# Attention scores from 128-row products instead of pairs of 64-row ones, on one Trainium2 core

## The chip, the cores and the metric

The kernel runs on one core of a Trainium2 chip. The metric is the device time of one execution in microseconds (us); the lower, the better. A core has a matrix engine (PE, with its weight loads shown apart as PEld), three engines for elementwise work (DVE, ACT and POOL), and a queue engine (SP) that here issues every transfer.

## The reference, cut to what matters

Attention with queries pooled in pairs, then two layers that share a shape: tokens times `w_in`, an activation, times `w_out`. All data are float32.

```python
# q, k, v: (2, 8, 1152, 64)
q_pool = q.reshape(B, H, S // 2, 2, D).mean(axis=3)          # 576 queries
scores = (1 / sqrt(D)) * matmul(q_pool, k.transpose(0, 1, 3, 2))
scores = scores - max(scores, axis=-1, keepdims=True)
attn = exp(scores)
attn = attn / (sum(attn, axis=-1, keepdims=True) + 1e-09)
x = matmul(attn, v)                                          # heads side by side: (1152, 512)
# layer 1: g = max(h, 0) + log1p(exp(-|h|)), h = x @ w_in    (512 -> 2048), x = g @ w_out
# layer 2: g = P(h) / (Q(h) + 1e-06),        h = x @ w_in2   (512 -> 2048), out = g @ w_out2
```

## The kernel before, in words

**Numbers in two halves.** Where a product must keep float32 accuracy at the fast matmul form (`F32R`), an operand is split: a rounded copy (hi, by `cp` on ACT, L317) and the rest (lo, by `sub` on DVE or POOL, L332). A product is then hi·hi + hi·lo + lo·hi.

**Attention.** There are 16 heads, and each head has two units of 288 queries (`unit`). A unit works on 9 blocks of 128 keys, with keys on partitions. `scores` (L529) multiplies halves of keys and queries that have 64 rows each: of a pair of blocks, one lies on rows 0 to 63 and the other on rows 64 to 127, three products each, so that a group has 6 matmuls (3 for the ninth block). ACT copies the scores from the PSUM banks to `s` (L317), DVE takes the running maximum over blocks (L543). PE turns the maxima (L492), DVE reduces them (L496), PE spreads them over the partitions (L502), DVE subtracts them from `s` (L561, `shift`: one operation of 4 blocks, one of 5), ACT takes the exponential (L567). Of the 9 blocks, `NF = 4` go to the product with the values as they are, in float32 (`pv_mm`, L598: two records of PE each in the trace); the other 5 are split (ACT, POOL) and need three fast matmuls each. The values carry a column of ones, so that the 65th row of the product is the divisor.

**Division.** `norm` has queries along the free dimension. The row of divisors goes by DMA to 64 partitions (L608), DVE takes the reciprocal (L614, L615), a DMA writes it to DRAM (`rr`), and a third brings it back to 64 partitions at 576 columns (L622). Then DVE multiplies (L628) and POOL splits into `xh` and `xl`.

**Halves of keys and queries.** PE turns them (`trans_k` L441, `trans_q` L455) into the bank `tp`; ACT writes hi and DVE lo straight to where `scores` reads them. The pooled queries are formed twice (768 columns, POOL, L418), so that a transpose yields them on both row halves.

**The two layers.** Weights come as 64-bit patterns, and three DVE operations of 512 columns each make float32 of them (`conv`: L676, L679, L682), ACT and POOL split them. `h_tile` (L718) and `out_part` (L800) are the matmuls; weights of layer 2 are converted during layer 1 and spilled to DRAM. The weights of layer 1 need place that the attention partly holds.

**What sets the order.** A planner (`Plan.order`) takes all operations with costs and due times (the tables `OFF`, `OFF2`, and `M0`, `WAIT`, `SLACK`) and writes one order for each engine; each engine then runs its own list in that order, and SP issues its transfers in order too.

Of the kernel before, what the change touches and what calls it, by code (L numbers as in the profile page):

```python
# [61 lines left out]
class Plan:  # L62
# [127 lines left out]
OFF = {  # L190
    'ld': -208.506,
    'sk': 456.792,
    'tk': -10.631,
    'tke': -22.672,
    'sq': 571.705,
    'tq': -9.202,
    'tqe': 57.498,
    'lv': 814.394,
    'sv': 472.654,
    'sc': 26.693,  # L200
    'ev': 239.369,
    'mx': -188.252,
    'mt': -512.124,
    'mr': -751.613,
    'mb': -496.324,
    'sh': 114.379,
    'ex': -235.892,
    'hi': 363.781,
    'lo': -129.074,
    'pv': 54.535,  # L210
    'pvs': -2.399,
    'po': -786.015,
    'nm': -944.097,
}
OFF2 = {
    'ld': 1068.049,
    'hi': 1032.528,
    'lo': 1261.355,
    'sp': -532.101,
    'ld2': -1028.1,  # L220
    '1a': 2.026,
    '1d': -491.462,
    '1y': -212.91,
    '1r': -107.908,
    '1z': -620.1,
    '1g': 349.501,
    'gh': -34.506,
    'gl': 7.815,
    '2h': -356.498,
    '2a': -41.673,  # L230
    '2t': -157.758,
    '2q': -160.224,
    '2b': 43.715,
    '2A': 44.626,
    '2m': 197.929,
    '2n': -37.418,
    '2r': 1055.77,
    '2g': -549.269,
    'out': 2034.143,
    'end': 220.812,  # L240
    'c1': -195.815,
    'c2': -141.646,
    'co': 16.527,
    's0': 65.606,
    's1': 21.449,
# [3 lines left out]
M0 = 295.089  # L249
QKT = 0.46  # L250
WAIT = 0.093
SLACK = 0.005
# [23 lines left out]
def fused_kernel(  # L276
# [20 lines left out]
    HW = SQ // 2  # L297
    NQ = HW // 96
# [39 lines left out]
    LF, LR = 93696, 78848  # L338
# [4 lines left out]
    NF = 4  # L343
# [16 lines left out]
    def lay_ps(phase, **what):  # L360
        for name, (bs, n) in what.items():
# [3 lines left out]
    kq = [("k1", 1, 2560), ("k2", 1, 2560), ("q1", 1, 2304), ("q2", 1, 2304)]  # L365
    r1 = lay(0, arena_r, 0, LR, *kq, *kq)
    r2 = lay(0, arena_r, r1, LR, ("vs", 2, NS * 768))
    r3 = lay(0, arena_r, r2, LR, ("ph", 2, NS * 1152), ("pl", 2, NS * 1152))
    f1 = lay(0, arena, 0, LF, ("kr", 2, 2560), ("qr", 2, 3072), ("qm", 1, 3072), ("vf", 2, 2368))
    f2 = lay(0, arena, f1, LF, ("s", 4, 10368))  # L370
    f3 = lay(0, arena, f2, LF, ("mx", 2, 1152), ("ud", 3, 2304), ("rb", 1, 2304), ("xp", 1, 2304), ("mp", 2, 2304), ("mc", 2, 32),
             ("dc", 2, 64), ("rc", 2, 64))
# [6 lines left out]
    lay(1, arena_r, 0, r3, *wch * 5, *g * 3)  # L379
    lay(1, arena_r, r3, LR, *wch * 3, *g)  # L380
# [6 lines left out]
    def attention():  # L387
        T = 7.4
        groups = [(0, NF), (NF, NS)]
        vfb = [P.buf("vf", [128, KC, VW], F32) for _ in range(2)]  # L390
        vsb = [P.buf("vs", [128, NS, 192], F32R) for _ in range(2)]
# [7 lines left out]

        def head(hd):  # L400
# [3 lines left out]
            first = hd == 0  # L404
            NQQ = 2 * NQ
            kr = P.buf("kr", [128, KC + 1, D], F32)
# [7 lines left out]
            qm = P.buf("qm", [96, NQQ, 2, D], F32)

            def pool_q():
                x = [qr()[:, :, r, :][:, :, None, :].to_broadcast([96, NQQ, 2, D]) for r in range(2)]
                (nc.vector if first else nc.gpsimd).tensor_tensor(out=qm(), in0=x[0], in1=x[1], op=ALU.add)  # L418

            e = "V" if first else "G"  # L420
            P.op(e, sub_t(e, 2 * NQQ * D), pool_q, r=[qr], w=[qm], at=t0 + OFF['sq'] * T)
            KP = (KC + 1) // 2
            kT = [P.buf("k1", [128, KP, 128], F32R), P.buf("k2", [128, KP, 128], F32R)]
            qT = [P.buf("q1", [128, SQ], F32R), P.buf("q2", [128, SQ], F32R)]
            spare = ["mT", "mB", "pv"] if first else []

            def halves(t, n, np_, src, dst, keys, at):

                hi, lo = dst
                P.op("A", act_t(n), lambda: cp("A", hi(), src()), r=[t], w=[keys[0]], at=at)  # L430
                P.op("V", dve_t(n), lambda: sub("V", lo(), src(), hi()), r=[t, keys[0]], w=[keys[1]], at=at)

            def trans_k(g):

                js = [(0, 1, 2), (3, 4)][g]
                t = P.buf(spare.pop() if spare else "tp", [128, 3, 128], F32)

                def mm():
                    for n, j in enumerate(js):
                        w = min(2, KC - 2 * j) * D  # L440
                        nc.tensor.transpose(  # L441
                            t()[0:w, n, :], kr()[:, 2 * j:2 * j + w // D, :].rearrange("p c d -> p (c d)"), ident)

                P.op("P", 0.11 * len(js), mm, r=[kr], w=[t], at=t0 + OFF['tk'] * T)
                for lo, hi, np_ in ((js[0], js[-1] + 1, 128),) if g == 0 else ((3, 4, 128), (4, 5, 64)):
                    halves(t, 128 * (hi - lo), np_, lambda lo=lo, hi=hi, np_=np_: t()[0:np_, lo - js[0]:hi - js[0], :],
                           [lambda x=x, lo=lo, hi=hi, np_=np_: x()[0:np_, lo:hi, :] for x in kT],
                           [(x, lo) for x in kT], t0 + OFF['tke'] * T)

            def trans_q(s):  # L450
                t = P.buf(spare.pop() if spare else "tp", [128, 3, 96], F32)

                def mm():
                    for j in range(3):
                        nc.tensor.transpose(  # L455
                            t()[:, j, :], qm()[:, 3 * s + j].rearrange("p i d -> p (i d)"), ident[:96, :96])

                P.op("P", 0.25, mm, r=[qm], w=[t], at=t0 + OFF['tq'] * T)
                halves(t, 288, 128, t,
                       [lambda x=x: x()[:, s * HW:(s + 1) * HW].rearrange("p (j c) -> p j c", j=3) for x in qT],  # L460
                       [(x, s) for x in qT], t0 + OFF['tqe'] * T)

            trans_q(0)
            trans_k(0)
            trans_k(1)
            trans_q(1)
# [3 lines left out]
            P.op("G", pool_t(NS * D, False), lambda: cp("G", vsb[p]()[:, :, 0:64], vfb[p]()[:, NF:KC, 0:64]),  # L470
                 r=[(vfb[p], 0)], w=[(vsb[p], 0)], at=t0 + OFF['sv'] * T)
            P.op("G", pool_t(NS * D), lambda: sub(
                "G", vsb[p]()[:, :, 128:192], vfb[p]()[:, NF:KC, 0:64], vsb[p]()[:, :, 0:64]),
                r=[(vfb[p], 0)], w=[(vsb[p], 0)], at=t0 + OFF['sv'] * T)
            ud = P.buf("ud", [65, SQ], F32)
            unit(hd, 0, kT, qT, ud)
            unit(hd, 1, kT, qT, ud)
            norm(hd, ud, t0)

        def unit(hd, hf, kT, qT, ud):  # L480
            p = hd % 2
            t0 = (2 * hd + hf) * T
            st = P.buf("s", [128, KC, HW], F32)
            mp = P.buf("mp", [128, 2, HW], F32)
            mx = P.buf("mx", [128, HW], F32)
            for j in range((KC + 1) // 2):
                scores(st, mp, mx, kT, qT, hf, j, t0)
            mT = P.buf("mT", [96, NQ, 128], F32)

            def max_t():  # L490
                for j in range(NQ):
                    nc.tensor.transpose(mT()[:, j, :], mx()[:, 96 * j:96 * j + 96], ident)  # L492

            P.op("P", pe_t(NQ, 128), max_t, r=[mx], w=[mT], at=t0 + OFF['mt'] * T)
            mc = P.buf("mc", [96, NQ], F32)
            P.op("V", dve_t(NQ * 128), lambda: nc.vector.tensor_reduce(out=mc(), in_=mT(), axis=AX.X, op=ALU.max),  # L496
                 r=[mT], w=[mc], at=t0 + OFF['mr'] * T)
            mB = P.buf("mB", [128, HW], F32)

            def max_b():  # L500
                for j in range(NQ):
                    nc.tensor.transpose(  # L502
                        mB()[:, 96 * j:96 * j + 96], mc()[:, j:j + 1].to_broadcast([96, 128]), ident[:96, :96]
                    )

            P.op("P", 0.26, max_b, r=[mc], w=[mB], at=t0 + OFF['mb'] * T)
            for g in range(2):
                shift(st, mB, g, t0)
            ph = P.buf("ph", [128, NS, HW], F32R)
            pl = P.buf("pl", [128, NS, HW], F32R)  # L510
            for g in (1,):
                p_split(st, ph, pl, g, t0)
            pv = P.buf("pv", [128, HW], F32)
            for n, (kind, c) in enumerate(
                [("f", c) for c in range(NF)] + [("h", c) for c in range(NF, KC)] + [("l", c) for c in range(NF, KC)]
            ):
                pv_mm(pv, st, ph, pl, p, kind, c, t0, n)
            P.op("A", act_t(HW), lambda: cp("A", ud()[:, hf * HW:(hf + 1) * HW], pv()[0:65, :]),
                 r=[pv], w=[(ud, hf)], at=t0 + OFF['po'] * T)
# [379 lines left out]
```

## Time and profile before

| | |
|---|---|
| median of 3 runs | 710.89 us (710.17 to 712.0) |
| profiled execution: its own time | 711.2 us |
| its span, first to last instruction | 709.4 us |
| busy share of PE, DVE, ACT, POOL | 97%, 86%, 80%, 74% |
| mean granted clock of PE | 0.982 of 2.4 GHz |

The profile is one execution. Its span is 1.8 us shorter than its time, and its time is 0.3 us over the median. A busy share is a mean over stages: attention fills the span to about 290 us, the layers the rest, so that a change to the attention is read from its own stretch.

### The profile page before, as it was taken

What the parts mean: (1) busy time and instruction counts of PE and PEld (TensorE: products, weight loads), DVE (VectorE), ACT (ScalarE), POOL (GpSimd) and SP (SyncE); (2) the same over time, 40 slices, a digit from 0 to 9 for tenths busy, and PEclk for the clock granted to TensorE, in tenths of its full rate; (3) what the DMA queues carried; (4) which work ended last, traced back from release to release, by engine and by line L of the source; (5) the groups of instructions that cost most, each with busy time, mean ns of one, the idle gap of its engine ahead of it and who ended that gap; (6) DMA issues with size and microseconds to landing.
All of it is one profiled execution on the core that took longest, in us unless ns stands there. A gap on an engine that the chain in (4) does not pass through costs nothing.

```text
span 709.4 us, 11978 instructions
## 1 busy us (share of the span) xinstructions
PE 689.3 (97%) x4164; PEld 583.8 (82%) x4164; DVE 609.4 (86%) x844; ACT 568.9 (80%) x1043; POOL 527.3 (74%) x481
## 2 busy tenths in 40 slices
PE   7999999999999999969999999999999999999997
PEld 6666666677777767759999999999988999988986
DVE  4799999899999998988353899999999988789897
ACT  4698888888888888857878887788877888976773
POOL 3246756565757556898776997889998789997764
PEclk8699999999999999989999999999999999999999
DMA  8122222222222122455011469898622012201011
GB/s 238 36 67 59 59 59 60 61 59 63 65 59 59 26 86 56 149 168 177 31 35 55 142 194 298 273 323 298 198 76 71 30 35 63 82 1 45 0 46 44
DMA packets 66668, 70.05 MB, mean 99 GB/s; under 512 B 24496, under 2 KB 50096, under 8 KB 66608
## 3 DMA queue, kind: packets, MB, share of 16 engines
q1 hardware_dynamic: 66608, 69.30, 31.8%
q8 instruction: 32, 0.52, 0.3%
q14 instruction: 28, 0.23, 0.1%
HBM read 58.46 MB, written 10.78 MB: 98 GB/s over the span
## 4 chain that ended last, share of the span: by engine, by line
PE 73%; DVE 10%; POOL 6%; DMA 4%; issue 3%; ACT 3%; SPq 0%; POOLq 0%; DVEq 0%; ACTq 0%
PE banks L718 21%; PE banks L800 20%; PE banks L598 15%; PE banks L529 11%; POOL arena_r L332 2%; DVE arena L543 2%; DMA arena<-rr 2%; PE banks L492 1%; PE banks L455 1%; PE banks L441 1%; ACT arena L317 1%; DVE banks L782 1%; POOL arena L332 1%; DMA arena<-in_moe_w_in_dram 1%; POOL arena L778 1%
## 5 line engine op out<-in xcount | busy, mean ns | idle before, releaser
L332 POOL TENSOR_TENSOR arena_r<-arena,arena_r 128x512 fp32r<-128x512 f32 (+2 forms) x112 | 201.5, 1804 | 91.8 <-ACT arena_r L317 84.4
L800 PE MATMUL banks<-arena_r 128*128 128x384 f32 (+1 forms) x1008 | 214.1, 361 | 6.4 <-ACT arena_r L317 5.6
L718 PE MATMUL banks<-xh,arena_r 128*128 128x384 f32 x768 | 210.3, 338 | 1.3 <-POOL arena_r L332 1.2
L800 PEld LDWEIGHTS banks<-arena_r 128*128 128x128 f32 x1008 | 181.0, 188 | 24.6 <-ACT arena_r L317 6.2
L718 PEld LDWEIGHTS banks<-xh,arena_r 128*128 128x128 f32 x768 | 140.8, 189 | 5.9 <-POOL arena_r L332 2.3
L317 ACT COPY arena<-banks 128x576 f32<-128x576 f32 (+4 forms) x213 | 114.8, 558 | 29.9 <-PE banks L529 15.9
L782 DVE RECIPROCAL banks<-arena 128x384 f32<-128x384 f32 x48 | 122.6, 2555 | 10.0 <-POOL arena L774 6.2
L718 PE MATMUL banks<-xl,arena_r 128*128 128x384 f32 x384 | 129.2, 336 | 0.0
L332 POOL TENSOR_TENSOR arena<-arena 128x384 f32<-128x384 f32 x96 | 98.1, 1024 | 18.2 <-ACT arena L752 13.6
L529 PE MATMUL banks<-arena_r 64*128 64x288 f32 x864 | 102.8, 330 | 4.5 <-DVE arena L543 1.8
L529 PEld LDWEIGHTS banks<-arena_r 64*128 64x128 f32 x864 | 70.9, 192 | 43.5 <-issue 13.4
L332 DVE TENSOR_TENSOR arena_r<-banks,arena_r 128x384 fp32r<-128x384 f32 (+3 forms) x176 | 84.1, 481 | 26.3 <-ACT arena_r L317 26.1
L317 ACT CAST arena_r<-banks 128x384 fp32r<-128x384 f32 (+3 forms) x176 | 73.3, 427 | 38.5 <-DVE banks L754 15.1
L543 DVE TENSOR_TENSOR arena<-banks,arena 128x576 f32<-128x576 f32 (+1 forms) x128 | 85.7, 670 | 15.3 <-ACT arena L317 10.8
L561 DVE TENSOR_TENSOR arena<-arena,banks 128x1152 f32<-128x1152 f32 x64 | 95.4, 1490 | 0.3 <-PE banks L502 0.3
L317 ACT CAST arena_r<-arena 128x512 fp32r<-128x512 f32 (+1 forms) x96 | 83.9, 887 | 8.5 <-DVE arena L682 6.3
L567 ACT ACTIVATE arena<-arena 128x1152 f32<-128x1152 f32 x64 | 82.8, 1294 | 2.6 <-DVE arena L561 2.3
L598 PE MATMUL banks<-arena_r 128*65 128x288 f32 (+1 forms) x480 | 81.2, 305 | 0.0
L598 PE MATMUL banks<-arena 128*65 128x288 f32 x256 | 78.6, 417 | 1.4 <-ACT arena L317 1.4
L718 PEld LDWEIGHTS banks<-xl,arena_r 128*128 128x128 f32 x384 | 72.6, 189 | 0.9
L598 PEld LDWEIGHTS banks<-arena_r 128*65 128x65 f32 (+1 forms) x480 | 59.9, 136 | 6.6 <-issue 5.7
L774 POOL TENSOR_TENSOR arena<-arena 128x384 f32<-128x384 f32 x48 | 48.8, 1017 | 21.7 <-ACT arena L768 21.3
(52 smaller groups left out, 872.2 us busy)
## 6 DMA issues: line engine op xcount, KB each, us to landing
arena<-in_moe_w_in_dram SPq DMA_DIRECT2D x32, 512.0 KB, 4.2
arena<-in_moe_w_out_dram SPq DMA_DIRECT2D x32, 512.0 KB, 4.2
sp<-arena SPq DMA_DIRECT2D x32, 256.0 KB, 3.5
arena<-sp SPq DMA_DIRECT2D x32, 256.0 KB, 3.1
arena<-in_q_dram SPq DMA_DIRECT2D x16, 288.0 KB, 3.1
arena<-in_k_dram SPq DMA_DIRECT2D x16, 288.0 KB, 3.3
arena<-in_v_dram SPq DMA_DIRECT2D x16, 288.0 KB, 3.6
arena<-rr SPq DMA_DIRECT2D x16, 144.0 KB, 3.0
```

The costliest lines, as they stand in the source:

```text
L317: nc.scalar.copy(o, i)
L332: e.tensor_tensor(out=o, in0=a, in1=b, op=ALU.subtract)
L441: nc.tensor.transpose(t()[0:w, n, :], kr()[:, 2 * j:2 * j + w // D, :].rearrange("p c d -> p (c d)"), ident)
L529: nc.tensor.matmul(out=ps()[:, i, 0:HW], lhsT=kT[a]()[64 * i:64 * i + 64, j, :], rhs=qT[y]()[64 * i:64 * i + 64, hf * HW:(hf + 1) * HW], s ...
L543: P.op("V", dve_t(m * HW), lambda: nc.vector.tensor_tensor(out=o(), in0=x(), in1=y(), op=ALU.max), r=r, w=w, at=t0 + (OFF['mx'] + 0.15 * j ...
L561: nc.vector.tensor_tensor(out=s, in0=s, in1=mB()[:, None, :].to_broadcast([128, n, HW]), op=ALU.subtract)
L567: nc.scalar.activation(out=s, in_=s, func=AF.Exp, scale=escale)
L598: nc.tensor.matmul(out=o, lhsT=w, rhs=x, start=first, stop=last, skip_group_check=True)
L718: nc.tensor.matmul(out=hp(), lhsT=w()[:, kk * 128:(kk + 1) * 128], rhs=x[:, kk, :], start=(kk == 0 and n == 0), stop=(kk == KD - 1 and n = ...
L774: P.op("G", pool_t(CW), lambda: nc.gpsimd.tensor_tensor(out=Q(), in0=t(), in1=ah(), op=ALU.add), r=[t, ah], w=[Q], at=a("2q"))
L782: P.op("V", (69 + 6.25 * CW) / 1e3, lambda: nc.vector.reciprocal(out=h(), in_=Q()), r=[Q], w=[h], at=a("2r"))
L800: nc.tensor.matmul(out=o()[:, 0:w_], lhsT=lt, rhs=rh, start=(f == 0 and n == 0), stop=(f == FG - 1 and n == 2),)
```

## The change

- **Scores.** Hi and lo of the keys of a block stand above each other on 128 rows (`kT`), those of the queries likewise in `q1` and, the other way round, in `q2`. A block then has two matmuls of 128 rows, which add all four products of halves, lo·lo among them. To bring halves to the other 64 rows, they are written to `kh`, `kl`, `qh`, `ql` first, and SP moves them by DMA: 8 moves for the queries of a head, 10 for the keys (`split`, `move`, L503). The pooled queries are formed once (384 columns). Head 0 does it without DMA (`split_first`).
- **Units** have 256 and 320 queries instead of twice 288.
- **Blocks split.** 6 blocks of 9 go to `pv_mm` in float32 and 3 are split (`CUTS`).
- **Maximum.** The subtraction is cut in three of 3 blocks, the middle one on POOL, which reads a copy of the maxima that ACT makes (`ms`).
- **Division** has queries on partitions: PE turns each unit's result (L702), DVE divides from PSUM (L709 to L711) into `xn`; for each pair of heads PE turns it back (L723), and ACT and DVE split it into `xh`, `xl`. No DMA is left in it.
- **Tables and layout.** All due times and the planner's two tolerances are new, and so are the places of buffers in SBUF.

```diff
-    'ld': -208.506,
-    'sk': 456.792,
-    'tk': -10.631,
...
+    'ld': -379.676,
+    'tk': -3.823,
+    'tke': -469.411,
...
-M0 = 295.089
-QKT = 0.46
-WAIT = 0.093
-SLACK = 0.005
+CUTS = ((3, "V", "f"), (3, "G", "f"), (3, "V", "s"))
+M0 = 431.22
+WAIT = 0.175
+SLACK = 0.021
...
+    HALF = ((0, 256), (256, SQ - 256))
...
-    lay(1, arena_r, 0, r3, *wch * 5, *g * 3)
-    lay(1, arena_r, r3, LR, *wch * 3, *g)
+    lay(1, arena_r, 0, r1, *wch * 3, wch[0])
+    EARLY = [*wch * 4, *wch[1:], *g * 4]
...
+            def move(dst, src, r, w, nbytes, at):
+                P.op("S", 0.5, lambda: nc.sync.dma_start(out=raw(dst()), in_=raw(src())), r=[r], w=[w], at=at,
+                     xfer=dma_t(nbytes))
+
+            for s in range(2):
+                for x, o, src in ((0, 0, qh), (1, 1, qh), (0, 1, ql), (1, 0, ql)):
+                    move(lambda s=s, x=x, o=o: qT[x]()[64 * o:64 * o + 64, h2 * s:h2 * s + h2],
+                         lambda s=s, src=src: src()[64 * s:64 * s + 64].rearrange("p j c -> p (j c)"),
+                         src, (qT[x], s, o), 73e3, t0 + OFF['qx'] * T)
...
+                    for y in range(np_ // 64):
+                        for src, o in ((kh, y), (kl, 1 - y)):
+                            move(lambda a=a, b=b, y=y, o=o: kT().rearrange("p (j y) c -> p j y c", y=2)[64 * o:64 * o + 64, a:b, y, :],
+                                 lambda a=a, b=b, y=y, src=src: src()[64 * y:64 * y + 64, a:b, :],
+                                 (src, a), (kT, a, y, o), n * 33e3, t0 + OFF['kx'] * T)
...
-                for x, (a, y) in enumerate(((0, 0), (0, 1), (1, 0))):
-                    for i in range(n):
+                for c in range(n):
+                    for i in range(2):
                         nc.tensor.matmul(
-                            out=ps()[:, i, 0:HW],
-                            lhsT=kT[a]()[64 * i:64 * i + 64, j, :],
-                            rhs=qT[y]()[64 * i:64 * i + 64, hf * HW:(hf + 1) * HW],
-                            start=(x == 0),
-                            stop=(x == 2),
+                            out=ps()[:, c, 0:hw],
+                            lhsT=kT()[:, c0 + c, :],
+                            rhs=qT[i]()[:, q0:q0 + hw],
+                            start=(i == 0),
+                            stop=(i == 1),
                         )
...
+            ms = P.buf("ms", [128, hw], F32)
+            P.op("A", act_t(hw), lambda: cp("A", ms(), mB()), r=[mB], w=[ms], at=t0 + OFF['mc'] * T)
...
+            for n, e, kind in CUTS:
+                shift(st, ms if e == "G" else mB, c0, n, e, hw, t0)
...
+            def turn():
+                for i in range(nt):
+                    nc.tensor.transpose(tp()[:, i, :], ud()[:, i * m:(i + 1) * m], ident[:VW, :VW])
...
+                den = tp()[:, :, D:VW]
+                nc.vector.tensor_scalar(out=den, in0=den, scalar1=1e-9, scalar2=None, op0=ALU.add)
+                nc.vector.reciprocal(out=rc(), in_=den)
+                nc.vector.tensor_tensor(out=xn()[0:m, i0:i0 + nt, D * o:D * o + D], in0=tp()[:, :, 0:D],
+                                        in1=rc().to_broadcast([m, nt, D]), op=ALU.mult)
```

**PE, in the middle of the attention.** Before, half a head there reads as follows (`banks` is all of PSUM, `arena` and `arena_r` the two areas of SBUF; L529 scores, L598 product with the values, L455, L492, L502 transposes).

```order
L529 MATMUL banks<-arena_r 128x288 x6
L492 MATMUL banks<-ident,arena 96x128 x3
L529 MATMUL banks<-arena_r 128x288 x6
L455 MATMUL banks<-ident,arena 128x96 x3
L598 MATMUL banks<-arena 65x288
L529 MATMUL banks<-arena_r 128x288 x6
L598 MATMUL banks<-arena 65x288
L502 MATMUL banks<-ident,arena 128x96 x3
L598 MATMUL banks<-arena 65x288
L529 MATMUL banks<-arena_r 128x288 x6
L598 MATMUL banks<-arena 65x288
L529 MATMUL banks<-arena_r 128x288 x3
```

And this is a stretch of the same length now (L631 scores, L684 product with the values, L702 and L723 the transposes of the division, L587 and L597 those of the maxima, L518 those of the keys).

```order
L723 MATMUL banks<-ident,arena 128x80 x4
L631 MATMUL banks<-arena_r 128x256 x8
L684 MATMUL banks<-arena 65x320 x3
L702 MATMUL banks<-ident,arena 128x65 x2
L631 MATMUL banks<-arena_r 128x256 x2
L631 MATMUL banks<-arena_r 128x320 x4
L684 MATMUL banks<-arena 65x320 x3
L587 MATMUL banks<-ident,arena 128x128 x2
L518 MATMUL banks<-ident,arena 128x128 x3
L631 MATMUL banks<-arena_r 128x320 x4
L597 MATMUL banks<-ident,arena 128x128 x2
```

A head has 54 score matmuls before and 36 now, 16 records of float32 products (8 blocks) before and 24 now, 30 `F32R` ones with the values before and 18 now, and 23 transposes before against 29 now (3 fewer of the queries, 6 of L702, and 6 of L723 for every second head). Between the first turning of the next head's keys (L518 x3) and its first score stand 14 matmuls of scores, 9 `F32R` ones with the values, 6 records of float32 products and 7 transposes; the scores of a head still come in 8 groups.

**SP, in the middle of the attention.** Before, a head has six transfers here: queries, values, keys, and three of the division. Now these rows stand there (L503 the moves, L544, L547, L553 the loads of queries, keys and values; in brackets what a row waits for, where `DMAHW` is the completion of the transfer that stands eight places ahead).

```order
L544 DMA arena<-in_q_dram 96x6x128 [waits DMAHW2_49,Pool_49]
L503 DMA arena_r<-arena_r 64x288 [waits DMAHW3_49]
L503 DMA arena_r<-arena_r 64x288 [waits DMAHW4_49]
L503 DMA arena_r<-arena_r 64x288 [waits DMAHW5_49]
L503 DMA arena_r<-arena_r 64x288 [waits DMAHW6_49]
L503 DMA arena_r<-arena_r 64x288 [waits DMAHW7_49]
L553 DMA arena<-in_v_dram 128x9x64 [waits DMAHW0_49,PE_49]
L765 DMA arena<-in_moe_w_in_dram 128x4x256 [waits DMAHW1_49,DVE_49]
L503 DMA arena_r<-arena_r 64x3x128 [waits DMAHW2_49,Activation_49]
L503 DMA arena_r<-arena_r 64x3x128 [waits DMAHW3_49]
L503 DMA arena_r<-arena_r 64x3x128 [waits DMAHW4_49,DVE_49]
```

A head now has 21 transfers there instead of 6; the moves of the keys stand behind the load of the values, which waits for PE.

**DVE, in the first heads.** Before, DVE converts one tile of weights in head 0 (L676, L679, L682), and the next L676 stands 360 rows further on, near the end of the attention. Now these rows stand early (L769, L772, L775 are the same three operations, L646 the maximum over blocks, L591 its reduction).

```order
L769 TENSOR_SCALAR banks<-arena 128x512
L772 SCALAR_TENSOR_TENSOR banks<-arena,banks 128x512
L646 TENSOR_TENSOR banks<-banks,arena 128x256
L775 SCALAR_TENSOR_TENSOR arena<-arena,banks 128x512
L646 TENSOR_TENSOR arena<-banks,arena 128x256
L769 TENSOR_SCALAR banks<-arena 128x512
L772 SCALAR_TENSOR_TENSOR banks<-arena,banks 128x512
L591 TENSOR_REDUCE arena<-banks 128x2
L775 SCALAR_TENSOR_TENSOR arena<-arena,banks 128x512
```

Seven tiles are converted in the first 180 rows of DVE, and the eighth follows at row 400 of 873.

## Rows read from the trace of the kernel before

**Rows 1.** Stretch, length, busy PE, PEld, DVE, ACT, POOL (instructions); clock; DMA share, GB/s.

```profile
8.50:30.00 21.50, 17.82 (x97) 12.25 (x98) 14.98 (x27) 12.10 (x21) 7.33 (x7) 0.60 0.50 118
92.60:270.30 177.70, 177.66 (x1292) 125.75 (x1292) 166.59 (x252) 157.24 (x241) 111.30 (x71) 1.00 0.22 61
270.30:317.70 47.40, 39.14 (x231) 31.54 (x229) 42.62 (x67) 34.52 (x59) 41.13 (x38) 0.97 0.43 130
317.70:500.00 182.30, 182.30 (x1035) 181.13 (x1036) 140.49 (x235) 146.41 (x316) 154.75 (x170) 0.99 0.57 184
500.00:709.40 209.40, 205.17 (x1031) 184.06 (x1029) 184.56 (x174) 161.22 (x318) 175.19 (x171) 1.00 0.16 54
```

**Rows 2.** Chain that ended last, from 151.62 to 252.71 us: shares by line.

```profile
by line: PE banks L598 51.1%; PE banks L529 32.9%; PE banks L455 4.7%; PE banks L441 4.1%; PE banks L492 3.9%; PE banks L502 3.5%
```

**Rows 3.** The same chain in order of time: start, us, what; one head.

```profile
168.42 1.86 PE banks L598 x13
...
173.70 0.25 PE banks L502 x3
173.95 0.49 PE banks L598 x2
174.44 0.60 PE banks L529 x6
...
175.67 0.59 PE banks L529 x3
176.26 0.40 PE banks L455 x3
176.66 1.05 PE banks L598 x8
...
179.44 0.33 PE banks L492 x3
...
180.04 0.99 PE banks L529 x12
```

**Rows 4.** Timeline of PE at 363 us (start, us, engine, what), and weight loads by line.

```profile
363.97 4.84 PE L800 MATMUL banks<-arena_r 128*128 128x384 f32 x27
368.65 0.33 PE L718 MATMUL banks<-xh,arena_r 128*128 128x384 f32 x1
...
L800 PEld LDWEIGHTS banks<-arena_r 128*128 128x128 f32 x1008 | 181.0, 188 | 24.6 <-ACT arena_r L317 6.2
```

**Rows 5.** Groups of ACT, POOL from 92.60 to 270.30: busy us, mean ns, idle before.

```profile
L317 ACT CAST arena_r<-arena 128x1440 fp32r<-128x1440 f32 x21 | 29.4, 1400 | 0.3
L567 ACT ACTIVATE arena<-arena 128x1440 f32<-128x1440 f32 x21 | 29.6, 1412 | 0.0
L567 ACT ACTIVATE arena<-arena 128x1152 f32<-128x1152 f32 x22 | 25.9, 1178 | 0.4 <-DVE arena L561 0.3
L317 ACT COPY arena<-banks 65x288 f32<-65x288 f32 x22 | 8.7, 394 | 4.2 <-PE banks L598 3.1
L332 POOL TENSOR_TENSOR arena_r<-arena,arena_r 128x1440 fp32r<-128x1440 f32 x22 | 72.6, 3300 | 62.1 <-ACT arena_r L317 61.7
```

**Rows 6.** Groups of DVE, converting weights: 0 to 270 us, then 270 to 336.

```profile
L676 DVE TENSOR_SCALAR banks<-arena 128x512 int32<-128x512 int32 x1 | 0.7, 694 | 0.5 <-DMA arena<-in_moe_w_in_dram 0.5
...
L676 DVE TENSOR_SCALAR banks<-arena 128x512 int32<-128x512 int32 x18 | 12.4, 688 | 0.3
```

**Rows 7.** Chain in order of time, 285 to 320 us, and the timeline of PE there.

```profile
294.75 4.53 DMA arena<-rr
...
317.70 1.60 PE L800 MATMUL banks<-arena_r 128*128 128x384 f32 x3 [4.59 <-ACT arena_r L317]
```

**Rows 8.** Transfers: median us to landing; then SP's own time for one issue.

```profile
arena<-in_v_dram SPq DMA_DIRECT2D x16, 288.0 KB, 3.6
...
arena<-arena SPq DMA_DIRECT2D x16, 2.2 KB, 1.8
...
133.69 0.42 SPq L411 DMA_DIRECT2D arena<-in_k_dram  x1
```

More of the change, by code (lines that the diff above doesn't have):

```diff
@@ L190 @@
 OFF = {
-    'ld': -208.506,
-    'sk': 456.792,
-    'tk': -10.631,
[L194 to L213, printed above, removed]
+    'ld': -379.676,
+    'tk': -3.823,
+    'tke': -469.411,
+    'sq': -467.9,
+    'tq': -5.738,
+    'tqe': -48.7,
+    'lv': 71.168,
+    'sc': -2.465,
+    'ev': 158.262,
+    'mx': -169.349,
+    'mt': -193.887,
+    'mr': 43.115,
+    'mb': -1038.227,
+    'sh': 91.53,
+    'ex': 238.985,
+    'mc': -19.848,
+    'hi': 64.032,
+    'lo': 48.004,
+    'pvl': -0.128,
+    'kx': -176.491,
+    'qx': 362.732,
+    'kl': -155.713,
+    'ql': -142.351,
+    'sv': 133.4,
+    'shg': 791.754,
+    'pv': 1.345,
+    'pvs': 4.652,
+    'po': -157.43,
+    'nt': 1.954,
+    'xt': -159.038,
+    'xs': 32.999,
+    'nm': -749.187,
 }
 OFF2 = {
[L216 to L245, printed above, removed]
+    'ld': 325.714,
+    'hi': 1009.738,
+    'lo': -88.364,
+    'sp': -265.548,
+    'ld2': 222.067,
+    '1a': -364.59,
+    '1d': 87.489,
+    '1y': -62.987,
+    '1r': -685.84,
+    '1z': -1311.809,
+    '1g': -725.816,
+    'gh': -135.693,
+    'gl': -780.345,
+    '2h': -594.095,
+    '2a': -166.237,
+    '2t': -563.581,
+    '2q': 152.453,
+    '2b': 172.662,
+    '2A': -142.791,
+    '2m': -117.394,
+    '2n': -615.61,
+    '2r': 47.678,
+    '2g': -467.048,
+    'out': 593.712,
+    'end': 297.738,
+    'c1': -41.208,
+    'c2': -60.504,
+    'co': 10.22,
+    's0': 469.998,
+    's1': 252.018,
 }
@@ L387, in attention @@
     def attention():
[L388 to L389 removed]
+        T = 6.8
         vfb = [P.buf("vf", [128, KC, VW], F32) for _ in range(2)]
@@ L410, in head @@
                 w=[qr], at=t0 + OFF['ld'] * T, xfer=dma_t(295e3))
-            P.op("S", 0.5, lambda: nc.sync.dma_start(
-                out=kr()[:, 0:KC, :], in_=k[b, h].rearrange("(p c) d -> p c d", c=KC)),
+            P.op("S", 0.5, lambda: nc.sync.dma_start(out=kr(), in_=k[b, h].rearrange("(p c) d -> p c d", c=KC)),
                  w=[kr], at=t0 + OFF['ld'] * T, xfer=dma_t(295e3))
[L414 to L418, printed above, removed]
@@ L450, in trans_q @@
[L450 to L461, printed above, removed]
@@ L474, in head @@
                 r=[(vfb[p], 0)], w=[(vsb[p], 0)], at=t0 + OFF['sv'] * T)
[L475 to L480, printed above, removed]
+            if h % 2 == 0:
+                xns[hd // 2] = P.buf("xn", [128, 6, 2 * D], F32)
+            for hf in range(2):
+                unit(hd, hf, kT, qT)
+            if h % 2:
+                x_out(xns[hd // 2], b, h // 2, t0)
@@ L504, in max_b @@
                     )
[L506 to L517, printed above, removed]
```

355 lines of the change are left out of this document (213 added, 142 removed).

## The prediction

> **What bounds the kernel now.** I read the stretches first, then the chain of waits, then single groups. In the stretches the reader is to see that PE is busy in 177.66 of 177.70 us in the middle of the attention, with DVE at 166.59, ACT at 157.24 and POOL at 111.30, and in 182.30 of 182.30 us in the layers behind it; only between them (270 to 318 us) does PE stand still for 8.3 us while DVE has 42.62 of 47.40 [rows 1]. A busy PE alone proves little, since ends of matmuls are modelled; but the chain that ended last runs through PE alone for six heads, 101.09 us or 16.85 a head [rows 2, 3], so that the starts themselves follow on each other without a wait. By its shares a head has 5.54 us of scores (L529), 8.61 of products with the values (L598) and 2.73 of transposes [rows 2].
>
> The third reading is what one instruction takes there [rows 3]. Eight fast products with the values of 288 columns take 1.05 us, 0.131 each; two float32 records take 0.49, 0.245 each. A score group of 12 takes 0.99 us, of 6 takes 0.60, and the group of 3 for the ninth block 0.59. So 6 more cost 0.39: two halves of 64 rows run side by side at 0.131 a pair, and each group pays 0.20 us on top. A head has 30 such pairs or singles in 8 groups: 3.93 + 1.6 us, which are the 5.54. Beside score groups other rows are dearer too: three transposes take 0.40 us right behind one and 0.25 elsewhere. In all, products with the values would be 30 x 0.131 + 16 x 0.245 = 7.85 and are 8.61; transposes would be 12 x 0.083 + 11 x 0.11 = 2.21 and are 2.73. Thus 1.6 + 0.76 + 0.52 = 2.9 us of a head belong to going into 64-row products and out again.
>
> A rule of the Trainium skill speaks against the change: TensorEngine Tiling (Array Packing), section Theoretical Speedup, gives up to twice the speed for contractions of 64 rows or fewer, and the same page, section Tiling Modes, says that changing the mode drains the engine. The pairs at 0.131 us agree with the first and the 0.20 us of each group with the second [rows 3]; by the first alone the change would cost six more slots a head, by both it gains.
>
> **The change, part by part.**
>
> *Scores.* 54 matmuls in 30 slots become 36 of 128 rows; 256 and 320 columns are 288 in the mean. No row of before shows such a matmul at 288 columns. From below stands 0.131 (fast products with 128 rows and 288 columns), from above 0.173 (27 matmuls of 384 columns with 128 x 128 weights in 4.68 us) [rows 3, 4]. Fewer columns take less there, so I take 0.131: 36 x 0.131 = 4.72 us, and 6.2 at the upper end.
>
> *Fewer blocks split.* Float32 records go from 16 to 24, `F32R` ones from 30 to 18: 24 x 0.245 + 18 x 0.131 = 5.88 + 2.36 = 8.24 against 7.85. This edit costs PE 0.4 us a head and pays ACT and POOL.
>
> *Transposes.* Three of 96 columns go, nine a head come; they are 65 to 128 columns wide, bounded by 0.083 and 0.11 each, nearer 0.083. 2.21 - 0.25 + 0.75 = 2.71 us.
>
> *Sum on PE.* 4.72 + 8.24 + 2.71 = 15.67 us a head if all the cost of the 64-row groups goes; 16.95, no gain, if what lies on the neighbours (1.28 us) stays. The neighbours are dear just where a score group stands beside them, so I let a fifth stay: 15.92. The gain is 0.93 us, over 16 heads **15 us** (bounds 0 and 19).
>
> *The other engines.* ACT is busy 14.9 us a head (157.24 of 177.70). Exponentials go from four to six; between 1152 and 1440 columns a column costs 0.81 ns, so 768 and 960 columns take 0.87 and 1.02, three each make 5.66 against 5.18. The rounded copies fall from 2 x 1.40 to some 1.86; one copy of queries less is -0.40; two copies of the maxima are +0.79; the split of the result, three pieces for two heads, is some +0.5 [rows 5]. That is +0.4: 15.3 of 15.9. DVE loses a third of its subtraction and the multiplication of 576 columns, and takes three small operations a unit; it falls below 14. POOL goes from 2 x 3.30 for lo to four operations of 768 or 960 columns at 2.3 ns a column, 7.9 us, and loses the split of the result: some 10 of 15.9. None but ACT is near PE. The 1.9 us that ACT idles now it idles mostly on PE and in gaps under 0.5 us, so I price it in the rivals.
>
> *The moves.* SP's issue takes 0.42 us and a head has 21 transfers [rows 8]: 9 of 15.9 us, hidden as long as each is ready in time. The tight one is the first part of the keys: 14 + 9 matmuls at 0.131, 6 records at 0.245 and 7 transposes, 5.2 us, stand between their turning and their first use. In that time lie the turning (0.33), a cast and a subtraction (some 0.5 each, by the rate of ACT's copies), two issues (0.84) and a landing, bounded by 1.8 us (2.2 KB inside SBUF) and 3.6 us (288 KB from DRAM) [rows 3, 5, 8]; a move has 96 KB, so some 2.4: 4.6 us, without the queue on ACT and DVE. I charge 0.1 us a head, **+2 us** (bounds 0 and +11, which is 0.7 a head).
>
> *The tail.* Before, one tile of weights is converted up to 270 us, and 18 from 270 to 336, at three operations of 0.69 us each [rows 6]. Now seven are done in the attention, where DVE has room: 6 x 2.06 = 12.4 us of DVE less in the stretch in which PE waits. The chain there runs through the last heads' transfers for the division (4.53 us for one) and ends in 4.59 us of PE waiting for weights [rows 7]; these transfers are gone as well. I take the 8.3 us that PE idles as the gain: **-8 us** (bounds -2, the transfers alone, and -13).
>
> *Start and layers.* Head 0 casts keys and queries before it turns them (two operations of some 0.6 us more in the chain), and head 1 needs 18 moves, 8 us of SP, at a time when PE is granted 0.60 of its clock in the mean, mostly the lower level of 1.2 GHz (8.5 to 30 us [rows 1]): **+1.5 us** (bounds 0 and +5). The layers have the same instructions, and PE has no idle time there to lose or win: 0 (bounds -1 and +4).
>
> *Sum.* -15 + 2 - 8 + 1.5 = -19.5, from the profiled execution's own 711.2 us: 691.7. The median is 0.3 below that execution, so the forecast is **691 us**. By its own terms it goes from 681 to 701.
>
> **The rivals.**
>
> *ACT sets the pace.* For it: 15.3 of 15.9 us leaves little, and ACT now idles 1.9 us a head in waits. Against it: DVE at 94% lets PE run full now [rows 1]. If a head takes 16.6 us, 4 us are won there: 711.2 - 4 + 2 - 8 + 1.5 = 702.
>
> *All of it comes.* 15.67 us a head (-19) and a tail without idle time (-13): 711.2 - 19 - 13 = 679.
>
> *The moves come late (slower).* Place: the first score of each head. Each us of wait costs 15 us; the gain of 22 us is gone at 1.5 us a head. With 2 us: 720. For it: 4.6 us of chain in 5.2 us, and the moves of the keys stand behind the load of the values, which waits for PE. Against it: no step of it is near its bound together with the others.
>
> *The 0.20 us belongs to a score group, not to its 64 rows (slower).* There are 8 groups a head still; with all 2.9 us staying a head takes 18.5, 1.7 more: 711.2 + 27 + 2 - 8 + 1.5 = 733. It decides from about 0.2 us a group on. Against it: groups of products with the values start behind other kinds as well and show 0.131 from the first [rows 3].
>
> *Weight loads don't hide.* A load of 128 x 128 takes 0.188 us; 36 of them beside the matmuls would add 6.8 us a head, some 800 us in all. Against it: the 27 matmuls take 0.173 each with their loads, less than a load alone [rows 4]. The Trainium skill, TensorE: Matmul & The Clock Gate, section Measured speedup vs the span model, says that loads overlap running matmuls only where the row group differs, which would be this rival; the trace does not agree, at 0.173 us.
>
> **How the numbers follow.** Forecast 0.62; ACT's pace 0.15 (702); all of it 0.10 (679); gains and waits cancel, 0.03 (711); late moves 0.05 (720); cost of the group 0.03 (733); loads 0.02. The range, 678 to 706, takes in the first three. A difference under 0.3% can't be told from none here. Faster 0.87, the same 0.03, slower 0.10.
>
> **What would show it.** Right: 36 score matmuls a head with starts 0.12 to 0.145 us apart and no 0.2 us at the head of a group; a head of 15.7 to 16.2 us; PE still above 98% busy in the middle and ACT near 95%; no idle stretch of PE over 2 us between attention and layers. Wrong: PE gaps at the first score of each head that end with a move (late moves), gaps that end with a copy of ACT (ACT's pace), or score matmuls at 0.17 us and more (loads).

## The result: 719.81 us, 1.2% slower

The changed kernel takes 719.81 us (median of four, 718.87 to 721.2) beside 711.15 us for the kernel before: ratio 1.0124, 95% interval 1.01 to 1.0148. The forecast was 691 us, so the sign is wrong. The span of the profiled execution is 717.2 us, 7.8 more than before. The first view is busy time by stretch; columns as in [rows 1].

```profile
8.50:30.00 21.50, 17.01 (x96) 12.61 (x95) 13.48 (x23) 13.69 (x27) 9.67 (x9) 0.84 0.77 191
97.00:256.60 159.60, 149.84 (x949) 114.10 (x947) 126.74 (x253) 133.44 (x251) 92.28 (x64) 1.00 0.49 119
256.60:300.00 43.40, 41.11 (x258) 31.34 (x258) 38.07 (x73) 34.02 (x63) 24.69 (x20) 1.00 0.42 118
300.00:350.00 50.00, 49.86 (x292) 46.43 (x291) 31.91 (x61) 41.86 (x88) 43.05 (x44) 1.00 0.28 85
350.00:500.00 150.00, 149.98 (x864) 149.25 (x862) 113.56 (x189) 119.27 (x260) 123.74 (x137) 1.00 0.57 181
```

The second row is nine heads. No engine is full there: PE 93.9%, ACT 83.6, DVE 79.4, POOL 57.8. Before, PE was full and DVE and ACT were busier than now [rows 1]. Every engine has less to do in a head than before, and the heads are longer.

Where the 7.8 us lie follows from the starts of the first score of each head (36 matmuls of L631 a head; 54 of L529 before). Up to head 5: 8.1 to 97.0 us, 88.9 against 84.1 before (+4.8). Heads 5 to 15: 97.0 to 277.8, 18.08 a head against 16.96 (+11.2; 4.0 of it in head 14, which holds 57 records of products with the values where the nine heads ahead of it hold 41 in the mean). The last head is 1.1 shorter and the start 0.4 earlier, so the last score falls at 291.7 instead of 277.2: +14.5. From there to the end it is 425.5 us instead of 432.2: -6.7. Eleven weight tiles are converted up to 291 us, and the fourth row shows PE at 49.86 of 50.00 where it stood still before [rows 7].

What PE does in a head was priced rightly. The spacing of score matmuls is 0.118 us at 256 columns and 0.146 at 320, 0.132 in the mean (forecast 0.131). Products with the values come to 0.215 and 0.270 in float32, 0.117 and 0.146 otherwise, 8.19 us a head (forecast 8.24). With the transposes PE needs about 15.6 us. The other 2.1 of 17.7 us (the nine heads) are waits. The busy row has 16.65 us a head, since the ends of matmuls are modelled; in another order (below) the same matmuls run in heads of 15.80 us. The view of waits for the same nine heads; columns are who waits, for whom, us in total, times, longest:

```profile
DVE arena L646 <- ACT arena L326: 14.6, 17, 1.4
ACT arena L326 <- DVE arena L646: 8.9, 17, 1.1
DVE arena L591 <- PE banks L587: 5.4, 11, 0.7
PEld banks L587 <- DVE arena L646: 5.4, 10, 1.1
ACT arena L326 <- DVE arena L341: 5.3, 8, 1.4
ACT arena L663 <- DVE arena L341: 4.5, 7, 1.2
PEld banks L631 <- ACT arena L326: 4.2, 11, 0.9
PEld banks L723 <- DVE arena L711: 4.0, 4, 1.3
...
PEld banks L631 <- DVE arena L646: 2.9, 6, 1.0
```

L326 is ACT's copy, L646 DVE's maximum over blocks, L341 DVE's subtraction, L711 the division. The first two rows are the odd ones: DVE waits for ACT and ACT for DVE, 23.5 us in both directions. In the timeline (start, length, what; idle time and who ended it in brackets) one such hand-over:

```profile
186.64 0.42 ACT L326 COPY arena<-banks 128x320 f32<-128x320 f32 x1
...
187.09 0.50 DVE L646 TENSOR_TENSOR banks<-banks,arena 128x320 f32<-128x320 f32 x1 [0.77 <-ACT arena L326]
...
187.62 0.49 DVE L646 TENSOR_TENSOR arena<-banks,arena 128x320 f32<-128x320 f32 x1
...
188.16 0.38 PEld L587 LDWEIGHTS banks<-ident,arena 128*80 128x80 f32 x4 [0.54 <-DVE arena L646]
```

Copy and maximum read the same score bank. The maximum starts 0.03 us after the copy's end, and PE stands for 0.54 us behind it. Over the whole trace I set the copy and the maximum of the same two blocks side by side: of 96 pairs none overlap, in 36 the maximum goes first and the copy waits, and in 75 the second starts within 0.1 us of the first's end (51 of 96 in the kernel before). The Trainium skill, PSUM — Partial Sum Buffer, section PSUM bank collisions raise a hardware error, says that two engines must not be at the same bank and partitions together, two readers included, and that the program has to keep them apart; the trace agrees, 0 of 96.

### The profile page after: what moved, and what is told of

It reads as the page before. It is cut to its first block, busy times and chain, and to the rows that moved or that the text cites. A ratio compares the mean times of both kernels' runs of the same rounds, so it can differ in the third digit from the quotient of the medians.

```text
span 717.2 us, 12195 instructions
## 1 busy us (share of the span) xinstructions
PE 684.7 (95%) x3921; PEld 594.8 (83%) x3921; DVE 576.4 (80%) x901; ACT 565.3 (79%) x1117; POOL 515.2 (72%) x482
## 4 chain that ended last, share of the span: by engine, by line
PE 59%; DVE 12%; ACT 9%; POOL 8%; issue 6%; DMA 4%; SPq 1%; ACTq 0%; DVEq 0%; POOLq 0%
PE banks L811 23%; PE banks L893 22%; PE banks L684 7%; DVE arena L646 5%; ACT arena L326 5%; DMA arena_r<-arena_r 4%; PE banks L631 3%; DVE arena L341 2%; ACT arena L663 2%; POOL arena_r L341 2%; ACT arena_r L326 2%; POOL arena L871 2%; POOL arena L867 1%; POOL arena L873 1%; SPq L503 1%
## 5 line engine op out<-in xcount | busy, mean ns | idle before, releaser
L341 POOL TENSOR_TENSOR arena<-arena 128x384 f32<-128x384 f32 (+2 forms) x128 | 162.7, 1276 | 60.7 <-ACT arena L326 46.5
L341 POOL TENSOR_TENSOR arena_r<-arena,arena_r 128x512 fp32r<-128x512 f32 (+3 forms) x112 | 156.5, 1403 | 55.3 <-ACT arena_r L326 51.0
L893 PEld LDWEIGHTS banks<-arena_r 128*128 128x128 f32 x1008 | 180.8, 188 | 15.2 <-ACT arena L326 0.4
L326 ACT COPY arena<-banks 128x512 f32<-128x512 f32 (+6 forms) x245 | 124.2, 541 | 41.2 <-DVE arena L646 14.2
L631 PE MATMUL banks<-arena_r 128*128 128x256 f32 (+1 forms) x576 | 110.5, 317 | 9.2 <-DVE arena L646 6.4
L341 DVE TENSOR_TENSOR arena_r<-banks,arena_r 128x384 fp32r<-128x384 f32 (+3 forms) x156 | 76.0, 488 | 52.5 <-ACT arena_r L326 51.8
L646 DVE TENSOR_TENSOR arena<-banks,arena 128x512 f32<-128x512 f32 (+3 forms) x128 | 86.9, 679 | 29.6 <-ACT arena L326 25.3
L684 PE MATMUL banks<-arena 128*65 128x256 f32 (+1 forms) x384 | 106.6, 416 | 3.6 <-ACT arena L326 2.8
L631 PEld LDWEIGHTS banks<-arena_r 128*128 128x128 f32 x576 | 82.7, 190 | 21.8 <-DVE arena L646 11.4
L663 ACT ACTIVATE arena<-arena 128x768 f32<-128x768 f32 (+1 forms) x96 | 86.9, 932 | 10.6 <-DVE arena L341 9.9
L326 ACT CAST arena_r<-banks 128x384 fp32r<-128x384 f32 (+3 forms) x160 | 67.5, 433 | 27.4 <-DVE banks L876 13.8
L684 PEld LDWEIGHTS banks<-arena 128*65 128x65 f32 x384 | 51.8, 140 | 34.6 <-ACT arena L326 4.5
L326 ACT CAST arena_r<-arena 128x512 fp32r<-128x512 f32 (+3 forms) x98 | 68.9, 722 | 9.5 <-DVE arena L434 2.8
L341 DVE TENSOR_TENSOR arena<-arena,banks 128x768 f32<-128x768 f32 (+1 forms) x64 | 66.8, 1043 | 3.5 <-PE banks L597 2.5
L867 POOL TENSOR_TENSOR arena<-arena 128x384 f32<-128x384 f32 x48 | 49.0, 1020 | 16.6 <-ACT arena L861 16.6
```

Of the source, the lines that this page charges most:

```text
L326: nc.scalar.copy(o, i)
L341: e.tensor_tensor(out=o, in0=a, in1=b, op=ALU.subtract)
L631: nc.tensor.matmul(out=ps()[:, c, 0:hw], lhsT=kT()[:, c0 + c, :], rhs=qT[i]()[:, q0:q0 + hw], start=(i == 0), stop=(i == 1),)
L646: P.op("V", dve_t(m * hw), lambda: nc.vector.tensor_tensor(out=o(), in0=x(), in1=y(), op=ALU.max), r=r, w=w, at=t0 + (OFF['mx'] + 0.15 * j ...
L663: P.op("A", act_t(n * hw, False), lambda: nc.scalar.activation(out=s(), in_=s(), func=AF.Exp, scale=escale), w=ks_, at=t0 + OFF['ex'] * T)
L684: nc.tensor.matmul(out=y, lhsT=w, rhs=x, start=(start and c == c0), stop=(stop and c == c0 + n - 1), skip_group_check=True)
```

## Theories

**Hand-overs.** ACT and DVE take turns at PSUM banks: score banks (copy and maximum) and the bank of the spread maxima (ACT's new copy for POOL and DVE's subtraction). A group of 640 columns holds its bank for 0.69 us of copy and 0.82 us of maximum one after the other. The planner that writes the order lets both run at once, so its order is too tight there. Before, PE's 16.85 us a head covered that; now PE is ready sooner. **Rivals:** the moves come late; DVE's or POOL's new work itself is too long; the parts cost the time in any order.

## Experiments

**Moves left out** (the order stays):

```diff
-P.op("S", 0.5, lambda: nc.sync.dma_start(out=raw(dst()), in_=raw(src())), r=[r], w=[w], at=at,
+P.op("S", 0.5, (lambda: nc.sync.dma_start(out=raw(dst()), in_=raw(src()))) if hd < 2 else (lambda: None),
```

> Leaves out the placing of halves from the third head on (scores are then taken from the halves of heads 0 and 1); the order of all other instructions is that of the changed kernel. Late-moves theory: a head falls from 17.65 us to 16.2 or less, 20 us or more in all, below 700. Hand-over theory (2 us a head lost in waits between PE, ACT and DVE on single banks): the moves end only some of these waits, 0 to 5 us, 715 to 720.

719.39 us, 1.0116 (1.0088 to 1.0145) of before, as with the moves. The row of the same nine heads:

```profile
97.00:256.60 159.60, 149.85 (x947) 114.08 (x947) 126.74 (x253) 133.44 (x250) 92.58 (x64) 1.00 0.20 52
```

The DMA share falls from 0.49 to 0.20, and PE, DVE and ACT are busy for the same time to 0.02 us. The moves cost nothing in this order; that rival falls.

**Maxima from the copy in SBUF:**

```diff
-top(mp, lambda: ps()[:, :, 0:hw], mp, 2, [ps], [mp])
+top(mp, lambda: st()[:, c0:c0 + 2, :], mp, 2, own, [mp])
```

> The maxima over blocks are taken from the copies in SBUF, so that ACT alone reads a score bank and DVE never waits for the bank. Hand-over theory: the waits of ACT for the maxima (8.9 us in nine heads) and of PE for banks that the maxima hold go, 6 to 12 us in all, 708 to 714. Late-moves theory: no change within 2 us.

779.88 us, 1.0972 (1.0933 to 1.1011). Groups of DVE there, and in the changed kernel below (count, busy us, mean ns):

```profile
L646 DVE TENSOR_TENSOR arena<-arena 128x512 f32<-128x512 f32 x24 | 30.6, 1276 | 3.1 <-ACT arena L326 2.6
L646 DVE TENSOR_TENSOR arena<-arena 128x640 f32<-128x640 f32 x21 | 30.2, 1437 | 3.2 <-ACT arena L326 2.8
```

```profile
L646 DVE TENSOR_TENSOR arena<-banks,arena 128x640 f32<-128x640 f32 x27 | 22.1, 820 | 8.0 <-ACT arena L326 6.3 <-PE banks L631 1.7
L646 DVE TENSOR_TENSOR arena<-banks,arena 128x512 f32<-128x512 f32 x27 | 18.6, 687 | 8.5 <-ACT arena L326 8.3
```

A missed expectation with a cause of its own: with both operands in SBUF the maximum takes 1276 instead of 687 ns. It says nothing on the theories, but it closes the easy way out of the shared bank.

**Another bank for the division's transposes:**

```diff
-tp = P.buf("tp", [m, nt, VW], F32)
+tp = P.buf("mT", [m, nt, VW], F32)
```

> The transposes of the division go to the bank of the maxima's transposes instead of the bank of the turning of keys and queries. Hand-over theory: part of the 7 us of PE waits in nine heads that end with the division or the split of the result goes, 4 to 10 us in all, unless the maxima's bank becomes the new place of the wait. Late-moves theory: no change within 2 us.

728.33 us, 1.0244 (1.022 to 1.0267): slower, and no theory expected that. The planner writes another order for it, so this run doesn't separate the bank from the order.

**The part on blocks undone:**

```diff
-CUTS = ((3, "V", "f"), (3, "G", "f"), (3, "V", "s"))
+CUTS = ((4, "V", "f"), (5, "V", "s"))
```

> Undoes the part on blocks: four blocks in float32 and five split, two stretches of subtraction both on DVE, no copy of the maxima for POOL. If the subtraction on POOL and its longer softmax chain cost the time: 10 us or more faster. Hand-over theory: within 5 us either way, since DVE gains 2 us of work a head and PE has 0.4 us less. Late-moves theory: within 3 us.

736.55 us, 1.0352 (1.0314 to 1.0389). In a stretch of attention DVE is now at 137.08 of 153.00 us, and PE at 144.12:

```profile
97.00:250.00 153.00, 144.12 (x975) 118.00 (x976) 137.08 (x248) 131.58 (x208) 75.10 (x42) 0.99 0.50 119
```

Outside the 5 us of the hand-over theory, and not the 10 us faster of the other. But heads 5 to 15 take 17.02 us there, less than the 18.08 of the changed kernel; the loss lies ahead of head 5 (97.4 us from the first score, instead of 88.9) and behind the last score (441.7 us instead of 425.5). The order is another again, and with POOL's subtraction ACT's copy of the maxima is gone too, so this run decides nothing on either. From here on most of the experiments keep the order or change the order alone.

**Score banks freed, same order.** The maxima read another bank, so that ACT alone reads a score bank:

```diff
-top(mp, lambda: ps()[:, :, 0:hw], mp, 2, [ps], [mp])
+w, free = hw // 2, mBs[-1]
...
+    out=cut(o(), m), in0=free()[:, 0:w][:, None, :].to_broadcast([128, 2 * m, w]), in1=cut(y(), m), op=ALU.max),
...
+top2(mp, mp, 2, [ps], [mp])
```

> The changed kernel in the same order with the same instructions, but from the third unit on the maxima over blocks read the bank of the spread maxima instead of the score bank, so that ACT's copy and DVE's maximum of a group stand in different banks (left out: the true maxima; those of the unit before stand in). Bank theory (copy and maximum of a group go one after the other, and the bank is held for the sum of the two): the head falls from 17.65 us to 15.7 to 16.4, 20 to 35 us in all, 685 to 700. Theory of DVE's work (the maxima, the division and the splits fill DVE in bursts, whatever they read): the same work stays, 714 to 720. Theory of the softmax chain (POOL's subtraction, the copy of the maxima): 714 to 720.

710.25 us, 0.9989 (0.9971 to 1.0008): 9.5 us faster than the changed kernel, less than the 20 expected. Heads 5 to 15 take 17.34 us instead of 18.08. DVE's and POOL's work is the same, so those theories, which gave 714 or more, don't fit; but score banks are only a part.

> The same edit in the kernel before, same order. Bank theory: PE was busy there without gaps and hides the same hand-overs, so 0 to 5 us are won, 706 to 711. If the hand-overs cost as much there as in the changed kernel, 20 us or more are won.

715.38 us, 1.006 (1.0041 to 1.0079): the kernel before loses 4 us by the same edit. The edit has a price: PE's spreading of the maxima (L505) waits for the maxima that now read its bank.

```profile
PEld banks L505 <- DVE arena L555: 6.3, 6, 1.1
DVE arena L555 <- PE banks L505: 4.9, 6, 0.8
```

Net of this price nothing is won in score banks before; what they would win without it the run doesn't show. The 9.5 us of the changed kernel are net of such waits too.

**The planner gets the rule** that a PSUM buffer in use is free for an engine only when the others have ended:

```diff
+if b.slot is not None and b.slot.mem is self.psum:
+    t = max([t] + [x for e, x in b.last.items() if e != eng])
```

> The changed kernel with the same parts and tables; only the planner that writes the order gets a rule more: ACT and DVE are not given one PSUM bank at the same time. Bank theory: the plan then spaces the score groups and the copy of the maxima as they run, 8 to 18 us faster than the changed kernel, 702 to 712. DVE and softmax theories: the order changes at random, 715 to 730.

733.93 us, 1.0317 (1.0292 to 1.0341): missed. Heads 5 to 15 do fall, to 16.95 us (120.6 to 290.1), but up to head 5 it takes 112.1 us instead of 88.9. From 20 to 70 us PE waits there for moves:

```profile
PE banks L637 <- DMA arena_r<-arena_r: 10.0, 7, 3.0
```

The later heads gain by the rule, and the first heads lose more than that. A rule alone is no test of the parts.

> The kernel before with the same rule in its planner. Bank theory: the order was right only by accident of PE's longer products, and PE is full: within 5 us of before, 706 to 716. If the rule alone is a better planner for any kernel: 700 or less.

729.62 us, 1.0264 (1.0241 to 1.0286), 19.55 us a head from head 5 to 15. Missed too: the order of the kernel before was not right by accident of slack alone; another order costs it 18 us.

**Another order, same parts.** The rule and other tables of due times, found by a search over plans that count the rule (a few lines of 60):

```diff
-    'mb': -1038.227,
+    'mb': -17.693,
-    'shg': 791.754,
+    'shg': 36.771,
-WAIT = 0.175
+WAIT = 0.153
```

> All parts of the changed kernel, the planner with the rule that ACT and DVE are not given one PSUM bank together, and other tables of due times (chosen so that such a plan keeps PE fed); only the order of the same instructions differs. Hand-over theory: what the change loses, it loses in the order, since PE's own work is 15.6 us a head: 15.7 to 16.4 us a head, 685 to 700 in all, faster than the kernel before. Theory that the parts themselves cost the time (more transfers, the division's small operations, POOL's subtraction): 710 to 725 in any order.

695.75 us, 0.9773 (0.9758 to 0.9789): faster than both. Ten heads, 100.3 to 258.3 us, 15.80 us each:

```profile
100.30:258.30 158.00, 157.33 (x1070) 128.93 (x1070) 137.75 (x279) 145.04 (x278) 99.42 (x69) 1.00 0.53 128
```

PE is at 157.33 of 158.00, and the chain runs through it again. A piece of that chain, eight score matmuls of 256 columns at 0.119 us and six float32 ones at 0.215:

```profile
163.39 0.48 PE banks L637 x4
...
164.75 0.95 PE banks L637 x8
165.69 0.28 PE banks L603 x4
165.97 0.33 PE banks L524 x3
166.30 1.29 PE banks L690 x6
```

The theory that the parts cost the time in any order (710 to 725) falls.

> The kernel before with the same rule and tables chosen in the same way, with the score groups at 0.66 us in the plan instead of 0.46. PE is full at 16.85 us a head, so only the stretch between attention and layers is open: 700 to 711. If order is worth as much in this kernel as in the changed one: 690 or less.

732.74 us, 1.0292 (1.0263 to 1.0322), missed by 22: my tables for the kernel before are worse than its own. So 0.9773 compares two orders that were not found with equal luck; it shows what the parts allow, not what they are worth.

**Score banks freed in the new order** (the edit of the maxima again)**, and POOL's share undone** (tables searched again):

```diff
-CUTS = ((3, "V", "f"), (3, "G", "f"), (3, "V", "s"))
+CUTS = ((3, "V", "f"), (3, "V", "f"), (3, "V", "s"))
```

> The reordered changed kernel with the maxima taken from the bank of the spread maxima, as before (left out: the true maxima), same instructions and order. Hand-over theory: the new order hides the hand-overs of score banks behind PE's work, so that freeing them wins no more than 2 us, and may lose some 4 as in the kernel before: 694 to 700. If the order won for another reason, the 9.5 us of the changed kernel are won here too: 684 to 688.

705.14 us, 0.99 (0.9879 to 0.992): 9.4 us slower than the new order itself, more than the 4 expected. In the changed kernel's order the same edit won 9.5. Part of its price shows here: the maxima now stand in the bank from which ACT copies for POOL, and from 102.3 to 250 us ACT's copies wait 8.7 us for them and the maxima 6.5 us for ACT. So nothing is won in this order, but the run doesn't show that score banks cost nothing in it.

> The reordered changed kernel with POOL's third of the subtraction given back to DVE and without the copy of the maxima for POOL, tables chosen again in the same way. DVE stands at 13.7 of 15.8 us a head in the reordered kernel and gets 2.1 more, so it is full: 700 to 712. If POOL's longer subtraction were what holds the softmax up: 692 or less.

709.81 us, 0.9972 (0.9956 to 0.9988), as expected. DVE has 154.04 of 160.70 us, and a head takes 16.07:

```profile
102.40:263.10 160.70, 158.53 (x1062) 128.13 (x1062) 154.04 (x299) 139.36 (x256) 57.20 (x50) 1.00 0.57 132
```

**The bank of the spread maxima freed, in the changed kernel's order:**

```diff
-cp("A", ms(), mB())
+cp("A", ms(), mx())
```

> The changed kernel in its own order; ACT's copy for POOL reads the unit's maxima in SBUF instead of the bank of the spread maxima (left out: the spread maxima in POOL's third), so that it no longer waits for DVE's subtraction in that bank. Hand-over theory: the waits of ACT for that subtraction (5.3 us in nine heads) and of POOL and PE behind it shrink, 3 to 8 us won, 712 to 717. If only score banks matter: within 2 us of the changed kernel, 718 to 722.

713.69 us, 1.0029 (1.0014 to 1.0044): 6.1 us won, within 3 to 8.

> The changed kernel in its own order with both edits: maxima from the other bank and ACT's copy from SBUF. Then ACT waits for DVE in no bank of scores or maxima. Hand-over theory: the sum of both or more, since the copy no longer meets the maxima in that bank either: 698 to 706. If what stays lost in the first edit is due to other things (division, order of the weights' conversion): 707 to 711.

699.45 us, 0.9817 (0.979 to 0.9844): 20.4 us won, more than the sum of the two, as expected. Here three of DVE's rows of the changed kernel (65, 67 and 71 of its order), with what each waits for, and the same rows of this one:

```
65 L646 TENSOR_TENSOR arena<-banks,arena 128x640 [waits Activation_49]
67 L646 TENSOR_TENSOR arena<-banks,arena 128x640 [waits DVE_49,Activation_49]
71 L646 TENSOR_TENSOR banks<-banks,arena 128x320 [waits DVE_49,Activation_49]

65 L658 TENSOR_TENSOR arena<-banks,arena 128x640
67 L658 TENSOR_TENSOR arena<-banks,arena 128x640 [waits DVE_49]
71 L658 TENSOR_TENSOR banks<-banks,arena 128x320 [waits DVE_49]
```

Instructions, order, columns and transfers are those of the changed kernel; in these rows the waits for ACT are gone. In the stretch of the nine heads the maxima wait 2.4 us for ACT instead of 14.6, and ACT no longer for the maxima (8.9 us). All engines there:

```profile
97.00:256.60 159.60, 155.64 (x1029) 124.64 (x1029) 136.65 (x275) 141.99 (x270) 98.37 (x68) 1.00 0.51 125
```

PE has 155.64 instead of 149.84 us, and more work of every engine is done in the same time. The edits also allow what the changed kernel can't do, a maximum ahead of the scores of its group and ACT's copy ahead of the spread maxima. That hardly happens: of the maxima in this stretch one of 59 of two blocks and three of 19 of the ninth block start before the modelled end of their scores, by 0.2 us at most, and two of 19 copies before the end of the spreading, by 0.5 at most. But 42 of the 59 overlap the copy of their group, where none of 54 did. So this run decides for the hand-overs.

## Why the prediction was wrong, step by step

*What bounds the kernel now:* right as a reading. PE was full, and a head followed PE's own starts. But it hid that ACT and DVE hand banks to each other tightly there too (51 of 96 pairs within 0.1 us); no row of the forecast shows two engines at one bank.

*Scores, blocks, transposes:* right, 15.6 us a head against the 15.67 forecast, and the cost of the 64-row groups is gone.

*Sum on PE* (15.92 us a head, -15 us): **this step failed, not as PE's work but as a head's time.** The forecast lets the two be the same because "None but ACT is near PE". That is true of busy time (ACT 83.6%, DVE 79.4%), but it puts the waits of ACT, DVE and PE for each other at nothing, and they are 2.1 us a head. The attention took +14.5 us up to the last score, where the forecast had -15 + 2 + 1.5 = -11.5. Showed in its place: 20.4 us of the changed kernel end when ACT and DVE need not take turns in two kinds of bank, and 24 with another order. The change itself added to the turns: a copy by ACT and two subtractions by DVE now meet in the bank of the spread maxima, which only DVE read before.

*The moves* (+2): nothing, and as a rival they were wrong for this order. That this rival gave 720 us, the measured time, is luck: without the moves the kernel takes 719.39. SP's issue of a move takes 0.59 us in the median rather than 0.42, the landing 2.3 us for 96 KB, near the 2.4 estimated. In the first heads of another order they do come late (10.0 us of PE waits).

*The tail* (-8): right. PE's gaps over 0.15 us between the last score and 320 us fall from 8.3 to 0.6 us. *Layers* (0): such gaps behind 320 us grow from nothing to 1.6 us, within the bounds; tail and layers together are -6.7. *Start* (+1.5): the first score is 0.4 earlier and the first five heads 4.8 longer, though the granted clock from 8.5 to 30 us is 0.84 instead of 0.60; I can't say how much of that is head 0 and 1 and how much the same hand-overs.

*Rivals.* ACT's pace (702) was nearest in kind: PE's gaps end with copies of ACT, as its sign said, but more of them with DVE, and ACT is at 84%. The price was not the busy time but the turns. The cost of the score group (733) and the weight loads (800) did not come: 0.118 and 0.146 us a matmul. The sentence of the Trainium skill that the forecast cites for the loads stands just ahead of the section that it names.

*The range.* The bounds of the sum's own terms add up to -33 and +18 us, 678 to 729, and not to the 681 to 701 that the forecast states. The measured time lies inside the wider bounds, but not for the reasons behind them: PE's work came out near the low bound, and the moves cost nothing.

*Open:* the freed run stays 3.7 us behind the new order. By their profiles its head 14 takes 21.4 us instead of 16.1, the nine heads ahead of that 0.3 us more each and the part behind the last score 3.1 us more, while its first five heads take 5.4 us less. What part of this belongs to the one bank that division and turning share is open; its run changed the order as well.

## What to carry to other kernels

An engine that is full can hide the waits among the others, as PE did before; before its work is cut, list which two engines meet in one PSUM bank and add their times instead of taking the longer. Judge parts and order apart: with an order that a planner writes, try the same parts in a second order before a part is called slow. To find such a cost, keep the order and take away what makes an instruction wait, as the freed banks did.

## What the runs showed of the hardware

DVE's maximum with both operands in SBUF was slowed while POOL worked: of those of 512 columns, 21 that met no tensor operation of POOL took 685 ns in the median, five that lay wholly beside such operations 1425 ns (693 to 2360), and the longest of the others 2618. With one operand in PSUM, in the changed kernel, 23 that lay wholly beside such operations took 677 to 692 ns. The Trainium skill, SBUF — State Buffer, section Who interferes with whom, says that a DVE instruction with two SBUF inputs contends with reads of GpSimd, and one with a single SBUF input, outside certain faster modes, doesn't; the runs agree but for one of the five (693 ns). The issue of a move within SBUF took SP 0.59 us in the median of 162, where the forecast had 0.42 from one load of keys [rows 8]. It isn't the moves alone: the loads of queries, keys and values in the same nine heads took 0.53 to 0.60. One move with its landing, the issue at the upper end:

```profile
198.76 0.62 SPq L503
199.38 0.05 issue
199.43 2.07 DMA arena_r<-arena_r
```
